# Sparse attention and a rational MLP on one core: one pool of PSUM banks, output matmuls in fours, two batches staged on 72 partitions

## The chip, the cores and the metric

The kernel runs on one core of a Trainium2 chip. The metric is the device time of one execution in microseconds. Before the change it is 473.31 us, the median of three runs (468.19 to 480.4). The core has TensorE (PE, with its weight loads as PEld), VectorE (DVE), ScalarE (ACT), GpSimd (POOL) and SyncE (SP). They run their own instruction queues in order and wait for one another on semaphores. TensorE writes to PSUM, eight banks of 512 float32 for each of 128 partitions; VectorE and ScalarE read it from there.

## The reference, cut to what matters

```python
# q, k, v: [8, 8, 576, 64]; heads 0-3 are local, heads 4-7 strided
scores = q @ k.T / sqrt(64)
mask_local   = (rel >= 0) & (rel < 32)                      # rel = query - key
mask_strided = (rel >= 0) & (query % 32 == key % 32)
attn = softmax(where(mask, scores, -1e9)) @ v               # per head
x = attn as [4608 tokens, 512]
h = x @ w_in                                                # [4608, 2048]
P = a0 + a1*h + a2*h^2 + a3*h^3
Q = 1 + |b0|*|h| + |b1|*h^2
out = (P / (Q + 1e-6)) @ w_out                              # [4608, 512], float32
```

## The kernel before

**Staging.** Each of eight batches has four local heads ("L") and four strided heads ("S"). q and k are needed with the head dimension on the partitions. For batches 2 to 7, GpSimd's queue issues DMAs that cast them into a bfloat16 copy in device memory (L391), and SyncE's queue issues transposing DMAs from there (L549). Batches 0 and 1 (`b < NPE`) take a shorter way: a casting DMA (L437) brings the raw rows into an MLP buffer h, on TP = 96 partitions of TW = 384 elements, TensorE transposes them with an identity (L489, and L520 for copies with the head halves exchanged), and ScalarE and VectorE copy the result out of PSUM (L501, L503, L532, L534). There, two neighbouring positions of the sequence share one column: 64 partitions each.

**Attention.** A batch has four units: local, strided, strided, local, two heads each. In every unit TensorE writes a mask and the scores into a pair of banks (L657 and L666 for local, L740 and L747 for strided); VectorE takes the negative maxima (L676, L754); TensorE adds them (L683, L761); ScalarE takes the exponential (L689, L767). The result P is transposed, by TensorE in batches 0 and 1 (L701, L779, copied out by L589 and L591) and by SyncE's DMA later (L707, L787). TensorE then multiplies by v into another pair of banks (L718, L804; the strided units' sums L796 go to a bank of their own), and VectorE normalises (L727, L729, L811, L815). `turn` transposes the batch's output (L615, L621), and ScalarE writes it into XT (L636), the MLP's input. In a strided unit the 36 positions of a class stand 8 columns apart in q and k, and L747 reads them with that step.

**MLP.** Tokens go in nine chunks of 512. `mlp1` makes h: 16 tiles of four matmuls (L840), each evicted by ScalarE (L846), in two groups of eight tiles. Nine VectorE instructions on 128 x 4096 elements (L858 to L880) and a logarithm and exponential on ScalarE (L863, L865) turn a group into P/Q. `mlp2` multiplies by w_out: four output tiles m, for each a step of eight matmuls per group (L903), then an eviction (L914; two of the last chunk's by L912) and a store (L921) from GpSimd's queue, in the last chunk from SyncE's.

**Order.** The code makes a list of operations with an engine, a planned duration and a key. `schedule` is a greedy planner: it gives each engine the ready operation with the lowest key. `emit` writes the order out with semaphores, so on the chip it is fixed. Attention's key is 576 b + 144 per unit, mlp1's 512 c + 1500 (1000 for c = 0) + 16 per tile, mlp2's 512 c + 2250 + 60 m.

**PSUM.** The eight banks are dealt out by purpose in rings, in program order: R_ps, two pairs, for scores and accumulators of attention and the transposes of staging (the last chunk's outputs too); R_ph, two banks, for mlp1 and the transposes of P; R_sm, one bank, for sums and `turn`; R_po, one bank, for mlp2. A ring's next tile waits until the tile of the same place is free.

Of the kernel before, what the change touches and what calls it, by code (L numbers as in the profile page):

```python
# [22 lines left out]
class Op:  # L23

    __slots__ = ("eng", "maker", "dur", "deps", "key", "dst", "dma", "gen", "ndep", "users",
                 "ready", "fin", "cnt", "idx", "know")
# [33 lines left out]

class Prog:
    ENG = ("pe", "act", "dve", "pool", "sp")
# [5 lines left out]
    def op(self, eng, maker, dur, key, r=(), w=(), m=(), dma=None, after=()):  # L68
        o = Op(eng, maker, dur, key, None, dma)
        o.idx = len(self.ops)  # L70
        for d in after:
            o.deps[d] = 1
        for t in r:
            for d in t.w:
                o.deps[d] = 1
        for t in w:
            for d in t.prev:
                o.deps[d] = 1
        for t in m:
            for d in t.w + t.r:  # L80
                o.deps[d] = 1
        for t in r:
            t.r.append(o)
        for t in w:
            t.w.append(o)
        for t in m:
            t.w = [o]
            t.r = []
        if dma is not None:
            assert len(w) == 1  # L90
            o.dst = w[0]
            o.gen = w[0].gen
            o.dst.ndma[o.gen] = o.dst.ndma.get(o.gen, 0) + 1
        o.deps.pop(o, None)
        self.ops.append(o)
        return o

    def schedule(self):
# [13 lines left out]
        left = len(self.ops)  # L112
        while left:
# [14 lines left out]
            _, _, o = heapq.heappop(avail[e])  # L128
            free[e] = t + o.dur
# [8 lines left out]
            left -= 1  # L138
            for u in o.users:
                lat = 0.07 if u.eng == o.eng else 0.15  # L140
# [101 lines left out]
def bass_strided_sparse_attn__then__act_rational_pade_kernel(nc, q, k, v, moe_w_in, moe_w_out, moe_a, moe_b, out):  # L242
# [8 lines left out]
    CH = 512  # L251
# [11 lines left out]
    TP = 96  # L263
# [56 lines left out]
    R_o = ring("os", 3, [128, Fout], f32)  # L320


    def ps(name, shape):
        return nc.alloc_psum_tensor(name, shape, f32)
    R_ps = Ring([Tile(f"ps{i}", ps(f"ps_s{i}", [128, 2, 512])) for i in range(2)])
    R_ph = Ring([Tile(f"ph{i}", ps(f"ps_h{i}", [128, 512])) for i in range(2)])
    R_sm = Ring([Tile("sm0", ps("ps_sm", [128, 512]))])
    R_po = Ring([Tile("po0", ps("ps_out", [128, 512]))])

# [142 lines left out]
    def loads_pe(b, key, tq, tk, after):  # L472
        for n in range(2):
            h = stage[b, n]
            hv = h.t[:, :, :].rearrange("p g c -> p (g c)")
            for i, (t, st_) in enumerate(((tq, T_q[b][n]), (tk, T_k[b][n]))):
                eng = ("act", "dve")[i]
                sl = R_ps.next()
                pv = sl.t.bitcast(bf)
# [3 lines left out]
                def tr(e, pv=pv, hv=hv, i=i):  # L483
                    r = None
                    for hh in range(HL):
# [5 lines left out]
                P.op("pe", tr, 1.2, key + 2 * n, r=[st_, h, T_c], w=[sl], after=after)  # L491

                def ev(e, pv=pv, t=t, n=n, eng=eng):
                    o = t.t[:, PRE + n * SW:PRE + n * SW + SW].rearrange(
                        "p (a h q j) -> p a h q j", a=2, h=2, j=NB)
                    r = None
                    for a in range(2):
                        oo = o[:, a]
                        ii = pv[:, a, 0:2 * SC].rearrange("p (h j q) -> p h q j", h=2, j=NB)
                        if eng == "act":  # L500
                            r = e.activation(oo, ii, AF.Copy)  # L501
                        else:
                            r = e.tensor_copy(oo, ii)  # L503
# [6 lines left out]
                sw = (R_po, R_sm)[i].next()  # L510
                sv = sw.t.bitcast(bf)

                def tr2(e, sv=sv, hv=hv, i=i):
                    r = None
                    for x in range(2):
                        for hh in range(2):
                            for j in range(NB):
                                c0 = (i * HL + 2 * x + hh) * TW + 128 * j + 64 * (1 - x)
                                o0 = hh * SC + TP * j
                                r = e.transpose(sv[64 * x:64 * x + 64, o0:o0 + TP], hv[0:TP, c0:c0 + 64],  # L520
                                                IDN[0:TP, 0:TP])
                    return r
                P.op("pe", tr2, 0.8, key + 1, r=[st_, h, T_c], w=[sw], after=after)

                def ev2(e, sv=sv, t=t, eng=eng):
                    r = None
                    for x in range(2):
                        d0 = 0 if x else PRE + 2 * SW
                        oo = t.t[64 * x:64 * x + 64, d0:d0 + PRE].rearrange("p (h q j) -> p h q j", h=2, j=NB)
                        ii = sv[64 * x:64 * x + 64, 0:PRE].rearrange("p (h j q) -> p h q j", h=2, j=NB)  # L530
# [56 lines left out]
    def evict(eng, o, i, dur, key, src, dst):  # L587
        if eng == "act":
            P.op("act", lambda e: e.activation(o, i, AF.Copy), dur, key, r=[src], w=[dst])  # L589
        else:  # L590
            P.op("dve", lambda e: e.tensor_copy(o, i), dur, key, r=[src], w=[dst])  # L591
# [15 lines left out]
    def turn(b, kind, src, key):  # L607
        for kk in range(2):
            sm = R_sm.next()
            sv = sm.t.bitcast(bf)  # L610
            if kind == "L":
                def tr(e, sv=sv, kk=kk):
                    r = None
                    for i in range(NR2):
                        r = e.transpose(sv[:, 128 * i:128 * i + 128], src.t[:, i, 128 * kk:128 * kk + 128], IDN[:, :])  # L615
                    return r
            else:
                def tr(e, sv=sv, kk=kk):
                    r = None
                    for i in range(NBK):  # L620
# [4 lines left out]
            for t0, t1 in cuts(b):  # L625
# [3 lines left out]
                if kind == "L":  # L629
                    i_ = sv[:, s0:s1].rearrange("p (j q c) -> p j c q", q=2, c=32)  # L630
                    o_ = XT[:, kk, c0:c0 + t1 - t0].rearrange("p (j c q) -> p j c q", q=2, c=32)
                else:
                    i_ = bass.AP(tensor=sv, offset=s0 // 16,
                                 ap=[[1024, 128], [1, (s1 - s0) // 16], [NR, NBK], [64, 2]])
                    o_ = XT[:, 2 + kk, c0:c0 + t1 - t0].rearrange("p (i k q) -> p i k q", k=NBK, q=2)
                P.op("act", lambda e, i_=i_, o_=o_: e.activation(o_, i_, AF.Copy), 0.25 + (t1 - t0) / 1000, key,  # L636
                     r=[sm], w=tiles)

    def attention(b, st):
# [5 lines left out]
        for kind, idx in (("L", 0), ("S", 0), ("S", 2), ("L", 1)):  # L645
            key = base + 144 * u
            u += 1
            sc = R_ps.next()
            pst = sc.t
            ng = R_ng.next()  # L650
            if kind == "L":
# [3 lines left out]
                def score(e, tq=tq, tk=tk, pst=pst, idx=idx):  # L655
# [19 lines left out]
                flat = pst[:, :, 0:W].rearrange("p a (r c) -> p a r c", c=KW)  # L675
                P.op("dve", lambda e, flat=flat, ng=ng: e.tensor_reduce(  # L676
                    ng.t[:, 0:2 * NR2].rearrange("p (a r) -> p a r", a=2), flat, axis=AX.X, op=Alu.max, negate=True),
                    1.2, key, r=[sc], w=[ng])

                def negm(e, ng=ng, pst=pst):  # L680
                    r = None
                    for j in range(2):
                        r = e.matmul(pst[:, j, 0:W], IDN[:, :],  # L683
# [6 lines left out]
                    pp.t[:, :, 0:KW].rearrange("p (a r) c -> p a r c", a=2), flat, AF.Exp, scale=0.125),  # L690
                    1.0, key, r=[sc], w=[pp])
                pt = R_ptL.next()
                if b < NPE:
                    for j in range(2):
                        ph = R_ph.next()
                        pv = ph.t.bitcast(bf)

                        def trp(e, pv=pv, pp=pp, j=j):
                            r = None
                            for i in range(NR2):  # L700
# [4 lines left out]
                              pv[0:KW, 0:128 * NR2], 0.7, key, ph, pt)  # L705
# [5 lines left out]
                acc = R_ps.next()  # L711

                def av(e, pt=pt, acc=acc, idx=idx):
                    r = None
                    for jj in range(2 * NR2):
                        par, r2 = jj % 2, jj // 2
                        for j in range(2):
                            r = e.matmul(acc.t[64 * par:64 * par + 64, j, 65 * r2:65 * r2 + 65],  # L718
# [6 lines left out]
                a4 = acc.t[:, :, 0:65 * NR2].rearrange("p a (r c) -> p a r c", c=65)  # L725
                r4 = rc.t[:, 0:2 * NR2].rearrange("p (a r) -> p a r", a=2).unsqueeze(3)
                P.op("dve", lambda e, r4=r4, a4=a4: e.reciprocal(r4, a4[:, :, :, 64:65]),  # L727
                     0.25, key, r=[acc], w=[rc])
                P.op("dve", lambda e, r4=r4, a4=a4, idx=idx: e.tensor_tensor(  # L729
                    xl.t[:, :, :].rearrange("p r (a x d) -> p x a r d", a=2, d=64)[:, idx], a4[:, :, :, 0:64],  # L730
# [6 lines left out]
            def score(e, tq=tq, tk=tk, idx=idx, pst=pst):  # L737
                r = None
                for j in range(2):
                    e.matmul(pst[:, j, 0:WS], IDN[:, :], MS[:, :], start=True, stop=False,  # L740
                             skip_group_check=True)
                for sl in range(NBK):
                    for j in range(2):
                        for par in range(2):
                            ap = [[QW, 64], [NBK, SB]]
                            off = 64 * par * QW + PRE + SW + (idx + j) * SC + 4 * (sl % 2) + sl // 2
# [6 lines left out]
            s4 = pst[0:NR, :, 0:WS].rearrange("p j (b c) -> p j b c", c=SB)  # L753
            P.op("dve", lambda e, s4=s4, ng=ng: e.tensor_reduce(  # L754
                ng.t[0:NR, :].rearrange("p (j b) -> p j b", j=2), s4, axis=AX.X, op=Alu.max, negate=True),
                0.85, key, r=[sc], w=[ng])

            def negm(e, ng=ng, pst=pst):
                r = None
                for j in range(2):  # L760
                    r = e.matmul(pst[0:NR, j, 0:WS], IDN[0:NR, 0:NR],  # L761
# [6 lines left out]
                pp.t[0:NR, :, 0:SB].rearrange("p (j b) c -> p j b c", j=2), s4, AF.Exp, scale=0.125),  # L768
                0.75, key, r=[sc], w=[pp])
            pt = R_ptS.next()  # L770
            if b < NPE:
                for j in range(2):
                    ph = R_ph.next()
                    pv = ph.t.bitcast(bf)

                    def trp(e, pv=pv, pp=pp, j=j):
                        r = None
                        for i in range(4):
# [6 lines left out]
                          pv[:, 0:512], 0.6, key, ph, pt)  # L785
# [5 lines left out]
            acc = R_ps.next()  # L791
            sm = R_sm.next()

            def av(e, pt=pt, acc=acc, sm=sm, idx=idx):
                for s8 in range(NBK):
                    e.matmul(sm.t[:, 2 * s8:2 * s8 + 2], pt.t[:, s8, :], ONE[:, :], start=True, stop=True,  # L796
                             skip_group_check=True)
                r = None
                for j in range(2):
                    for g in range(4):  # L800
                        for par, mm in ((0, 64), (1, SB)):
                            for x in range(2):
                                c0 = 64 * (4 * j + g)
                                r = e.matmul(acc.t[64 * par:64 * par + mm, x, c0:c0 + 64],  # L804
# [4 lines left out]
            P.op("pe", av, 0.75, key, r=[pt, vS, T_one], w=[acc, sm])  # L809
            rc = R_rc.next()  # L810
            P.op("dve", lambda e, rc=rc, sm=sm: e.reciprocal(rc.t[0:NR, 0:16], sm.t[0:NR, 0:16]),  # L811
                 0.25, key, r=[sm], w=[rc])
            for j in range(2):
                h = idx + j
                P.op("dve", lambda e, rc=rc, acc=acc, h=h, j=j: e.tensor_tensor(  # L815
                    xsb.t[0:NR, :, 64 * h:64 * h + 64].rearrange("p (x g) d -> p x g d", x=2),
                    acc.t[0:NR, :, 256 * j:256 * j + 256].rearrange("p x (g d) -> p x g d", g=4),
                    rc.t[0:NR, 8 * j:8 * j + 8].rearrange("p (g x) -> p x g", x=2).unsqueeze(3).broadcast_to(
# [7 lines left out]
    def mlp1(c):  # L826
# [4 lines left out]
        for g in range(NG):  # L831
            h = R_h.next()
            for f in range(g * G, g * G + G):
                ph = R_ph.next()
# [156 lines left out]
```

## Time and profile before

The profiled execution took 466.26 us, of which the span, from its first to its last instruction, is 464.5 us.

| stretch, us | PE busy | DVE busy | ACT busy | DMA engines' busy share |
|---|---|---|---|---|
| 0 to 15 | 4.82 | 6.47 | 3.84 | 1.19 |
| 15 to 30 | 11.30 | 5.43 | 4.11 | 1.27 |
| 30 to 45 | 10.68 | 6.67 | 5.41 | 1.38 |
| 45 to 60 | 13.65 | 4.87 | 8.84 | 1.12 |
| 75 to 90 | 10.91 | 12.91 | 8.97 | 0.01 |
| 90 to 105 | 11.93 | 13.21 | 7.36 | 0.10 |
| 105 to 120 | 15.00 | 6.07 | 7.93 | 0.97 |
| 165 to 180 | 12.79 | 7.58 | 6.60 | 0.94 |
| 210 to 225 | 12.80 | 10.64 | 10.11 | 1.16 |
| 285 to 300 | 14.48 | 14.93 | 8.97 | 0.24 |
| 390 to 405 | 13.68 | 14.89 | 11.61 | 0.13 |

Each row is a window of 15 us with the busy time of the engines inside it. A DMA share over 1 comes from packets that overlap on an engine. In the page, a line such as "ng L754 <- PE ps_s L747: 8.6, 5, 3.3" means that an engine stood idle before line 754 until line 747 of TensorE had ended: 8.6 us in all, 5 times, 3.3 at the longest.

### The profile page before, as it was taken

The numbers are of one execution on the slowest core, as the hardware profiler recorded it, in microseconds if no ns is written. First come the engines' busy times: TensorE is split into PE (matmuls) and PEld (weight loads), VectorE is DVE, ScalarE is ACT, GpSimd is POOL, SyncE is SP. The second block draws the span as 40 slices with busy tenths as digits, with TensorE's granted clock in tenths as the row PEclk, the third lists the DMA queues.
The fourth block names the chain that finished last, engine by engine and source line by source line (L and its number), as shares of the span: only waits on it lengthen the run. The fifth ranks groups of instructions, "written<-read, shape, count | busy, mean of one in ns | idle before, by whom it ended". The sixth has DMA issues, their size and how long they took to land.

```text
span 464.5 us, 8489 instructions
## 1 busy us (share of the span) xinstructions
PE 382.7 (82%) x3752; PEld 193.5 (42%) x3752; DVE 358.6 (77%) x311; ACT 283.8 (61%) x308; POOL 71.8 (15%) x112
## 2 busy tenths in 40 slices
PE   3586959589967979979699899899979788987970
PEld 2354424355425535535354444444434333433430
DVE  3443298982977939996879689979988989999940
ACT  3223684745655828567386677769578588788520
POOL 9921010001311111211022003101000000100100
PEclk9999997669978979999899799989989899999996
DMA  9999982019998997899997546210400010100101
GB/s 115 207 191 216 187 146 53 1 24 165 155 147 170 182 168 147 167 173 122 109 164 152 103 88 126 75 24 24 97 23 24 23 45 7 63 23 24 65 22 73
DMA packets 101829, 47.46 MB, mean 102 GB/s; under 512 B 88512, under 2 KB 97728, under 8 KB 101312
## 3 DMA queue, kind: packets, MB, share of 16 engines
q0 software_dynamic: 20384, 27.04, 31.3%
q1 hardware_dynamic: 81408, 19.87, 26.4%
q8 instruction: 29, 0.48, 0.4%
q14 instruction: 8, 0.07, 0.1%
HBM read 40.18 MB, written 18.28 MB: 126 GB/s over the span
## 4 chain that ended last, share of the span: by engine, by line
DVE 37%; PE 33%; ACT 14%; DMA 7%; SPq 3%; issue 3%; POOL 1%; DVEq 0%; POOLq 0%
PE ps_h L840 14%; DVE u L862 6%; PE ps_out L903 5%; DVE z L870 4%; DVE z L868 4%; ACT u L865 4%; ACT u L863 4%; DVE u L860 3%; DVE z L858 3%; DVE h L880 3%; DVE z L866 3%; DMA tk<-tk 3%; DVE z L869 2%; PE ps_s L747 2%; ACT h L846 2%
## 5 line engine op out<-in xcount | busy, mean ns | idle before, releaser
L840 PE MATMUL ps_h<-XT,Win 128*128 128x512 bf16 x576 | 149.6, 409 | 12.5 <-ACT h L846 11.8
L846 ACT ACTIVATE h<-ps_h 128x512 bf16<-128x512 f32 x144 | 84.3, 600 | 63.5 <-PE ps_h L840 63.3
L903 PE MATMUL ps_out<-Wout,h 128*128 128x512 bf16 x512 | 119.4, 382 | 3.6 <-ACT os L914 3.6
L840 PEld LDWEIGHTS ps_h<-XT,Win 128*128 128x128 bf16 x576 | 53.7, 103 | 86.7 <-ACT h L846 26.5
L903 PEld LDWEIGHTS ps_out<-Wout,h 128*128 128x128 bf16 x512 | 49.3, 99 | 63.0 <-ACT os L914 6.1
L863 ACT ACTIVATE u<-u,consts 128x4096 bf16<-128x4096 bf16 x18 | 66.7, 3703 | 8.0 <-DVE u L862 8.0
L921 POOL DMA_DIRECT2D out_dram<-os x32 | 24.7, 771 | 265.9 <-ACT os L914 262.0
L865 ACT ACTIVATE u<-u 128x4096 bf16<-128x4096 bf16 x18 | 65.3, 3625 | 0.0
L858 DVE TENSOR_SCALAR z<-h 128x4096 uint16<-128x4096 uint16 x18 | 22.0, 1223 | 27.1 <-ACT h L846 27.1
L870 DVE TENSOR_TENSOR z<-z,h 128x4096 bf16<-128x4096 bf16 x18 | 41.1, 2282 | 0.5
L868 DVE TENSOR_TENSOR z<-z,h 128x4096 bf16<-128x4096 bf16 x18 | 41.1, 2283 | 0.4
L862 DVE TENSOR_TENSOR u<-u,z 128x4096 bf16<-128x4096 bf16 x18 | 41.0, 2277 | 0.3
L880 DVE TENSOR_TENSOR h<-z,u 128x4096 bf16<-128x4096 bf16 x17 | 38.9, 2287 | 0.8 <-ACT u L865 0.5
L914 ACT ACTIVATE os<-ps_out 128x512 f32<-128x512 f32 x32 | 19.3, 603 | 26.6 <-PE ps_out L903 26.6
L636 ACT ACTIVATE XT<-ps_sm 128x576 bf16<-128x576 bf16 (+2 forms) x40 | 21.4, 560 | 17.3 <-PE ps_sm L621 9.5
L676 DVE TENSOR_REDUCE ng<-ps_s 128x10 bf16<-128x960 f32 x16 | 18.5, 1154 | 14.9 <-PE ps_s L666 14.9
L689 ACT ACTIVATE pL<-ps_s 128x960 bf16<-128x960 f32 x16 | 15.5, 970 | 20.0 <-PE ps_s L683 20.0
L860 DVE TENSOR_SCALAR u<-z,coef 128x4096 bf16<-128x4096 bf16 x18 | 24.2, 1344 | 0.4
L866 DVE TENSOR_SCALAR z<-h,coef 128x4096 bf16<-128x4096 bf16 x18 | 24.0, 1335 | 0.3
L869 DVE TENSOR_SCALAR z<-z,coef 128x4096 bf16<-128x4096 bf16 x18 | 23.1, 1281 | 0.4
L871 DVE TENSOR_SCALAR z<-z,coef 128x4096 bf16<-128x4096 bf16 x18 | 23.0, 1278 | 0.3
L747 PE MATMUL ps_s<-tk,tq 64*36 64x36 bf16 x512 | 20.7, 245 | 0.0
(74 smaller groups left out, 365.2 us busy)
## 6 DMA issues: line engine op xcount, KB each, us to landing
out_dram<-os POOLq DMA_DIRECT2D x32, 256.0 KB, 2.5
q<-in_q_dram POOLq DMA_DIRECT2D x12, 288.0 KB, 5.1
k<-in_k_dram POOLq DMA_DIRECT2D x12, 288.0 KB, 6.5
vS<-in_v_dram POOLq DMA_DIRECT2D x16, 144.0 KB, 7.6
vL<-v SPq DMA_DIRECT2D x24, 96.0 KB, 4.3
Win<-in_moe_w_in_dram POOLq DMA_DIRECT2D x8, 256.0 KB, 11.5
Wout<-in_moe_w_out_dram POOLq DMA_DIRECT2D x4, 512.0 KB, 22.4
v<-in_v_dram POOLq DMA_DIRECT2D x6, 288.0 KB, 5.9
```

The lines of the kernel that those rows point to most:

```text
L840: r = e.matmul(ph.t[:, :], Win[:, kk, f * 128:(f + 1) * 128], XT[:, kk, xc:xc + CH], start=(kk == 0), stop=(kk == NK1 - 1))
L846: P.op("act", lambda e, f=f, ph=ph, h=h: e.activation(h.t[:, f % G, :], ph.t[:, :], AF.Copy), 0.6, key, r=[ph], w=[h])
L858: dv(lambda e, hh=h.t, zz=z.t: e.tensor_scalar(zz.bitcast(u16)[:, :, :], hh.bitcast(u16)[:, :, :], 0x7FFF, None, op0=Alu.bitwise_and), ts ...
L860: dv(lambda e, zz=zz, uu=uu: e.tensor_scalar(uu, zz, b1_ap, b0_ap, op0=Alu.mult, op1=Alu.add), ts + 0.28, r=[z, T_b], w=[u])
L862: dv(lambda e, zz=zz, uu=uu: e.tensor_tensor(uu, uu, zz, op=Alu.mult), tt, r=[z], m=[u])
L863: P.op("act", lambda e, uu=uu: e.activation(uu, uu, AF.Ln, bias=eps1, scale=1.0), 0.833 * W / 1000 + 0.28, key, r=[T_co], m=[u])
L865: P.op("act", lambda e, uu=uu: e.activation(uu, uu, AF.Exp, scale=-1.0), 0.833 * W / 1000 + 0.19, key, m=[u])
L866: dv(lambda e, zz=zz, hh=hh: e.tensor_scalar(zz, hh, a_ap[3], a_ap[2], op0=Alu.mult, op1=Alu.add), ts + 0.28, r=[h, T_co], m=[z])
L868: dv(lambda e, zz=zz, hh=hh: e.tensor_tensor(zz, zz, hh, op=Alu.mult), tt, r=[h], m=[z])
L870: dv(lambda e, zz=zz, hh=hh: e.tensor_tensor(zz, zz, hh, op=Alu.mult), tt, r=[h], m=[z])
L880: dv(lambda e, zz=zz, hh=hh, uu=uu: e.tensor_tensor(hh, zz, uu, op=Alu.mult), tt, r=[z, u], m=[h])
L903: r = e.matmul(pot, h.t[:, j, m * 128:(m + 1) * 128], Wout[:, kk, :], start=(kk == 0), stop=(kk == NF - 1))
```

## The change

- **One pool.** PSUM is one tensor. A tile of the new class `PTile` says only its kind and how many banks it needs: "at" (attention and staging, two neighbouring banks), "ph", "sm", "po" (one each). It has no bank until the planner orders its first operation. Quotas limit the open tiles: three at, three ph, two sm, four po. If there is no room, the operation is set aside until a tile closes, and another is ordered. The new holder's first operation waits for all operations of the bank's last holder.
- **Outputs in fours.** `mlp2` cuts each group of eight into two steps of four matmuls, and its four output tiles are separate tiles from the start. The steps of one tile keep their order.
- **72 partitions.** Staging of batches 0 and 1 uses TP = 72, so TW = 512 and a row of a transpose covers four columns (NB = 4 instead of 3). For the strided half the copy out of PSUM sorts columns by class, so that L747 reads 36 neighbouring columns in these two batches.
- **Smaller edits.** The strided sums are a step of their own. L815 is cut by bank (x) and not by head (j). The ring of output buffers os has four instead of three. L840 waits for the former users of h itself. Some planned durations are changed, and the planned latency between operations of one engine is 0 instead of 0.07.

The diff, cut:

```diff
+class PTile(Tile):
+    def __init__(self, kind, need):
+        Tile.__init__(self, kind)
+        self.need = need
+        self.banks = None
+        self.ops = []
+        self.left = 0
...
+    QUOTA = {"at": 3, "ph": 3, "sm": 2, "po": 4}
...
+        def room(o, t):
+            want = [p for p in o.pts if p.banks is None]
+            if not want:
+                return t
+            if any(nopen[p.name] + 1 > self.QUOTA[p.name] for p in want):
+                return None
+            n = want[0].need
+            assert len(want) == 1
+            spots = [list(range(i, i + n)) for i in range(9 - n) if not any(held[i:i + n])]
+            if not spots:
+                return None
+            if want[0].name in ("at", "ph") and 8 - sum(held) - n < 1 and nopen["po"] + nopen["sm"] < 1:
+                return None
+            when = [max(bank_free[i] for i in b) for b in spots]
+            at = min(when)
+            if at > t + 1e-9:
+                return at
...
+            for p in want:
+                p.banks = late
+                nopen[p.name] += 1
+                for i in p.banks:
+                    held[i] = True
+                    if bank_tile[i] is not None:
+                        for d in bank_tile[i].ops:
+                            o.deps[d] = 1
+                    bank_tile[i] = p
+            return t
...
             _, _, o = heapq.heappop(avail[e])
+            at = room(o, t)
+            if at is None:
+                o.ready = max(o.ready, t)
+                blocked.append(o)
+                continue
+            if at > t:
+                heapq.heappush(pend[e], (at, o.key, o.idx, o))
+                continue
...
-                lat = 0.07 if u.eng == o.eng else 0.15
+                lat = 0.0 if u.eng == o.eng else 0.15
...
-    TP = 96
+    TP = 72
...
-    R_o = ring("os", 3, [128, Fout], f32)
-    R_ps = Ring([Tile(f"ps{i}", ps(f"ps_s{i}", [128, 2, 512])) for i in range(2)])
-    R_ph = Ring([Tile(f"ph{i}", ps(f"ps_h{i}", [128, 512])) for i in range(2)])
-    R_sm = Ring([Tile("sm0", ps("ps_sm", [128, 512]))])
-    R_po = Ring([Tile("po0", ps("ps_out", [128, 512]))])
+    R_o = ring("os", 4, [128, Fout], f32)
+    PTile.PS = nc.alloc_psum_tensor("PSUM", [128, 8 * 512], f32)
+    PTile.PSB = PTile.PS.bitcast(bf)
...
+                            if n:
+                                o2 = oo[:, hh * SC:hh * SC + SC].rearrange("p (z j i) -> p z j i", z=2, j=NB)
+                                i2 = ii[:, hh * SC:hh * SC + SC].rearrange("p (j i z) -> p z j i", z=2, j=NB)
...
-                            ap = [[QW, 64], [NBK, SB]]
-                            off = 64 * par * QW + PRE + SW + (idx + j) * SC + 4 * (sl % 2) + sl // 2
+                            n = 4 * (sl % 2) + sl // 2
+                            ap = [[QW, 64], [1 if b < NPE else NBK, SB]]
+                            off = 64 * par * QW + PRE + SW + (idx + j) * SC + n * (SB if b < NPE else 1)
...
-                o = P.op("pe", mm, 0.9, key, r=[xt, T_win[f // G]], w=[ph])
+                o = P.op("pe", mm, 0.9, key, r=[xt, T_win[f // G]], w=[ph], after=h.prev)
...
+        for h, p0, p1, tp in groups:
+            for p in range(p0, p1, 4):
+                parts.append((h, p, min(p + 4, p1), tp))
+        groups = parts
+        pos = [PTile("po", 1) for m in range(CH // 128)]
```

## The prediction, as it was put on record

> **What bounds the kernel now.** I read the page's totals first (VectorE's row is its busy tenths in 40 slices), then the busy time by stretch.
>
> ```profile
> span 464.5 us, 8489 instructions
> ...
> PE 382.7 (82%) x3752; PEld 193.5 (42%) x3752; DVE 358.6 (77%) x311; ACT 283.8 (61%) x308; POOL 71.8 (15%) x112
> ...
> DVE  3443298982977939996879689979988989999940
> ```
>
> ```profile
> 0.00:55.10 55.10, 36.91 (x442) 22.63 (x443) 18.58 (x38) 18.13 (x28) 26.80 (x45) 1.00 1.25 183
> 55.10:445.00 389.90, 338.74 (x3279) 167.78 (x3278) 337.51 (x271) 264.49 (x278) 44.95 (x67) 0.92 0.51 93
> 445.00:464.50 19.50, 7.08 (x32) 3.05 (x32) 2.53 (x4) 1.19 (x2) 0.00 (x0) 0.78 0.14 54
> ```
>
> In the stretch rows the fourth and fifth figures are TensorE's and VectorE's load and busy time as PEld and DVE: VectorE works 18.6, 337.5 and 2.5 us. Its polynomial rows cannot shrink here, so I do the bookkeeping on VectorE: span = 358.6 busy + 105.9 idle, and the idle splits into 36.5 (start, 55.1 - 18.6), 52.4 (middle, 389.9 - 337.5) and 17.0 (end). The change touches no polynomial instruction; its worth is the idle that it removes.
>
> Next the waits, asked for VectorE from 105 to 270 us, and the rows of VectorE's timeline with long gaps (bracket: idle before, and who ended it).
>
> ```profile
> DVE ng L676 <- PE ps_s L666: 12.0, 6, 4.4
> DVE ng L754 <- PE ps_s L747: 8.6, 5, 3.3
> DVE z L858 <- ACT h L846: 6.1, 5, 1.8
> DVE rc L811 <- PE ps_s L804: 5.5, 3, 2.6
> DVE rc L727 <- PE ps_s L718: 4.9, 4, 2.9
> ```
>
> ```profile
> 55.10 1.23 DVE L858 TENSOR_SCALAR z<-h 128x4096 uint16<-128x4096 uint16 x1 [13.11 <-ACT h L846]
> ...
> 114.03 1.16 DVE L676 TENSOR_REDUCE ng<-ps_s 128x10 bf16<-128x960 f32 x1 [3.99 <-PE ps_s L666]
> ```
>
> These five add to 37.1 us: VectorE starves on attention results between 105 and 270. The same question for 270 to 445 gives 9.6 us at L858 and 0.5 at L880; the remaining 5.2 of the 52.4 are small gaps and the stretch 55 to 105. Ending the start is the first L858, at 55.10. So three places: the start, 105 to 270, and a little later on.
>
> **The start.** Timeline, attention of batch 0:
>
> ```profile
> 17.41 0.99 PE L666 MATMUL ps_s<-tk,tq 64*32 64x96 bf16 x36
> ...
> 18.45 1.16 DVE L676 TENSOR_REDUCE ng<-ps_s 128x10 bf16<-128x960 f32 x1 [0.31 <-PE ps_s L666]
> ...
> 20.68 0.97 ACT L689 ACTIVATE pL<-ps_s 128x960 bf16<-128x960 f32 x1 [4.36 <-PE ps_s L683]
> ...
> 22.80 0.68 PE L740 MATMUL ps_s<-MS,IDN 128*128 128x288 bf16 x2
> ...
> 23.42 1.29 PE L747 MATMUL ps_s<-tk,tq 64*36 64x36 bf16 x32
> ```
>
> R_ps has two pairs, handed out in program order score, accumulator, score, accumulator. So the next unit's score (L740, 22.80) needs the pair that the exponential L689 leaves at 21.65, though TensorE had ended its score at 18.40. With up to three pairs given out by need, that score can start some 4.4 us earlier. From 16.48 to the first L840 at 44.96 are 28.5 us; TensorE's groups in it add to 22.7 (two local units of 5.0, two strided of 4.75, four turns of 3.15 in all). So 5.8 us is all that overlap can take at this matmul pace. The class-ordered half adds to that: L747 takes 1.29 per 32 matmuls here and also at 209.94, whatever the pace; L804, with unit step and the same 32 matmuls, takes 0.64 at the slow pace and 0.44 at the fast one. Two scores lie in the start: 2 x 0.65 = 1.3. Upper end: if TensorE stays busy, its pace doubles (a group of four 128x512 needs 0.43 us per matmul at 45 us and 0.216 at 51), which adds perhaps 2. I take -5, ends +1 and -9.
>
> **Staging on 72 partitions.** The columns streamed stay (16 x 72 = 12 x 96); the transposes go from 144 to 192. A group of 12 takes 1.14 slow or 0.68 fast, so each costs 0.057 to 0.095: the 48 new ones cost between 0 (column-bound) and 4.6 us in all, half of it in the start, where TensorE waits 2.13 us for h at 13.98 anyway. Evicting the strided half takes four instructions of 288 instead of two of 576, eight more in all; the fixed part is bounded by the smallest PSUM row (reciprocal, 217 ns): four on VectorE, +0.9. Four transfers of h carry the same 288 KB in 288 rows instead of 384. The first landed 6.75 us after issue (1.30 to 8.05); fewer, longer rows could save up to a quarter, fewer partitions cost up to a third of what moves: -1 to +2 on the path. I take +1 for all of this.
>
> [...]
>
> **105 to 270.** Not all of the 37.1 is open to banks. TensorE itself waits for transposing DMAs in that stretch: tk at L657 7.7, P at L796 3.5, tk at L740 2.7, about 14, and DMA is 0.84 to 1.16 busy in most of those windows. That part stays. 23 is open: between 105 and 118, VectorE idles 9 us because batch 1's attention ended late (its last turns at 104) and chunk 1's mlp1 only then could start. Its units queue on two pairs as batch 0's did, and L740 waits 2.4 us for L689 at 70.4. Earlier attention also issues the next loads earlier: POOL stands from 69 to 107 at an output store (38.06 us, ended by L914), while DMA share is 0.01 to 0.10 from 75 to 105; splitting mlp2 in fours and giving it more banks releases that store and what is queued behind it. Batch 1's two contiguous scores save 1.3 more. I take two thirds, -15; ends +5 and -23.
>
> **270 to 445.** TensorE waits 29.7 us for mlp1's banks (20.0 load + 9.7 matmul, L840 behind L846) and 9.4 for the only output bank (L903 behind L914). Three ph banks and up to four output banks cover most of it, but VectorE is 94% busy, so only its 10.1 us of waits can go. I take -4, ends 0 and -10.
>
> **End and rest.** The last L912 waits 1.63 us for an os buffer; a fourth removes it, and next the last of four store issues (3.19 us together from 451.45) is late: -1, ends 0 and -1.6. L815 regrouped keeps 32 instructions of 512 elements (682 ns), the sums as their own step keep their matmuls: 0. L840 now waits for the old users of h on TensorE; the eviction L846 waited for them already, and the last of them are TensorE's own L903: 0, cover lost only if an h buffer is short, in which case attention queued behind L840 waits too, with VectorE after it. Fours add boundaries, not steps. [...]
>
> Sum: -5 + 1 - 15 - 4 - 1 = -24. Span 440.5, with the 1.76 outside it (466.26 - 464.5) 442.3. The profiled run lies 1.5% under the median of 473.31; scaled the sum would be 449. I predict 446. Own range: all lower ends (-9 -1 -23 -10 -1.6) give an own time of 421.7, all upper ends (start +1, staging +2 DMA +2.3 transposes +0.9 evictions, middle +5) 477.5; I take 424 to 464 of it.
>
> **Rivals.**
> - *Output banks starve attention (slower).*
>
> ```profile
> 78.39 1.89 PE L903 MATMUL ps_out<-Wout,h 128*128 128x512 bf16 x8
> ...
> 104.65 1.46 PE L903 MATMUL ps_out<-Wout,h 128*128 128x512 bf16 x6
> ```
>
> Today the single output bank sits half summed for 26 us, until the second group's h is there. The planner fills any idle TensorE time with what is ready, so all four output tiles can be opened with the first group, and four banks stay held. Four remain: one pair for attention if mlp1 takes two. Then units run one after the other: the first local unit takes 16.48 to 26.53, the first strided 22.80 to 32.27, so four take 39 us against 28.5, +10.5 a batch. For it: the hold and the greedy plan. Against: attention ranks ahead of the same period's output steps, and from batch 2 on P's transposes need no banks. Two batches cancel the gain of 24; from three on it is slower: four give 464.5 + 42 - 24 = 482.5, scaled about 491. Chance 0.18.
> - *DMA and VectorE hold the middle (no change).* If 105 to 270 is set by loads, -15 becomes 0 to -5 and the sum is -9 to -14: 452 to 457, scaled 459 to 464; with the start not gained either, 470. For it: the DMA windows. Against: the DMA hole at 75 to 105. Chance 0.22, of which 0.04 still counts as over 2%.
> - *The plan is not what the chip does.* Banks change hands by planned durations; where an eviction is late, TensorE stands with all queued behind it, giving back what the third pair gives. This lies inside +5 at the middle term: about 465 to 475, within 2%. Chance 0.02.
>
> **How the numbers follow.** Forecast 0.58. A difference under 2% cannot be told from none. Faster 0.58 + 0.04 = 0.62, within 2% 0.20, slower 0.18. Range 424 to 480: it leaves out most of the slower rival and the case of every gain at its end.
>
> **What would show it.** First L858 near 50 instead of 55; L740 of the second unit before L689 of the first; L747 of batches 0 and 1 at 0.5 to 0.7 us per 32; VectorE's waits from 100 to 270 near 20 us; the last L912 without a DMA wait. It is wrong if the output bank's first and second four are 15 us apart on four tiles at once while L676 waits for L666, or if h lands later than 8 us.

## The result and the profile after

The changed kernel takes 440.14 us (median of four runs, 435.48 to 441.54), where the kernel before takes 472.0 (four runs, 468.19 to 480.4). The ratio is 0.9333, 95% interval 0.9227 to 0.9439. The forecast was 446, a ratio of 0.942 to the first median of 473.31. The two profiled runs took 466.26 and 441.54. Single runs of one program lie up to 15 us apart in this study, so whole times are compared by ratios of the means of the fast runs with their intervals, and traces by places that repeat.

The page's totals of the changed kernel, in the columns of before:

```profile
span 439.8 us, 8607 instructions
...
PE 368.9 (84%) x3800; PEld 186.4 (42%) x3800; DVE 361.0 (82%) x315; ACT 284.7 (65%) x312; POOL 69.9 (16%) x112
...
DVE  3471799999983257899999999999999999999930
```

VectorE works 2.4 us more than before, so its idle time fell by 27.1 us for a span that is 24.7 shorter. The row of tenths shows where it stands idle now: at the start, once around the 13th to 15th slice (132 to 165 us), and at the end. Three stretches follow: up to the first L965, the first VectorE instruction on a group (L858 before), called the first product below; from there to the start of the last 32 output matmuls; and the rest. In each row the third pair of figures after the length is VectorE's busy time:

```profile
0.00:46.62 46.62, 30.69 (x488) 18.41 (x489) 18.38 (x40) 17.86 (x31) 27.22 (x45) 0.93 1.40 170
46.62:418.83 372.21, 328.97 (x3287) 164.40 (x3283) 340.08 (x273) 265.68 (x280) 42.66 (x67) 0.94 0.57 103
418.83:439.80 20.97, 9.27 (x32) 3.59 (x32) 2.53 (x4) 1.19 (x2) 0.00 (x0) 0.66 0.14 51
```

VectorE's idle time is the length less the busy time. The end begins with the last 32 output matmuls, at 445.0 before and 418.83 after:

| VectorE, us | before | after | difference |
|---|---|---|---|
| busy | 358.6 | 361.0 | +2.4 |
| idle in the start | 36.5 | 28.2 | -8.3 |
| idle in the middle | 52.4 | 32.1 | -20.3 |
| idle at the end | 17.0 | 18.4 | +1.5 |

**The start.** Rows of batch 0 on TensorE (PE) and ScalarE (ACT):

```profile
15.31 0.99 PE L765 MATMUL PSUM<-tk,tq 64*32 64x96 bf16 x36
...
17.14 0.99 PE L765 MATMUL PSUM<-tk,tq 64*32 64x96 bf16 x36
...
19.08 0.97 ACT L788 ACTIVATE pL<-PSUM 128x960 bf16<-128x960 f32 x1 [7.17 <-PE PSUM L782]
...
24.67 0.42 PE L841 MATMUL PSUM<-MS,IDN 128*128 128x288 bf16 x2 [0.37 <-DVE tk L601]
...
25.02 0.57 PE L849 MATMUL PSUM<-tk,tq 64*36 64x36 bf16 x32
...
26.01 0.57 PE L849 MATMUL PSUM<-tk,tq 64*36 64x36 bf16 x32
```

The second unit's score (17.14) no longer waits for the first one's exponential (19.08). The planner chose the other local unit, whose operands need only the first half of q and k. The strided scores read neighbouring columns and take 0.57 us where they took 1.29. TensorE is also at its faster pace by then: the mask matmuls L841 take 0.42 us where L740 took 0.68. And attention begins 2.1 us earlier, at 14.40 (L756) instead of 16.48 (L657), because the transposes of the strided half, at 13.98 and 15.56 before, now come behind it, at 20.62 and 22.34.

**The middle.** VectorE's waits from 100 to 270 us, and its busy time in five stretches:

```profile
DVE ng L856 <- PE PSUM L849: 14.4, 2, 10.3
DVE rc L919 <- PE PSUM L899: 6.4, 2, 4.5
DVE rc L827 <- PE PSUM L818: 3.4, 3, 2.0
DVE ng L775 <- PE PSUM L765: 2.4, 2, 1.9
DVE xS L922 <- PE PSUM L912: 0.2, 1, 0.2
```

```profile
46.62:96.50 49.88, 42.51 (x561) 23.53 (x558) 48.67 (x48) 36.15 (x44) 1.54 (x3) 0.93 0.60 102
96.50:120.00 23.50, 23.50 (x254) 12.44 (x253) 23.22 (x19) 15.64 (x16) 5.68 (x9) 1.00 0.88 166
120.00:161.50 41.50, 29.61 (x403) 16.29 (x405) 19.66 (x24) 19.02 (x26) 7.01 (x12) 0.75 1.04 152
161.50:261.50 100.00, 94.58 (x1102) 48.56 (x1103) 93.57 (x78) 74.59 (x81) 15.51 (x24) 0.97 0.88 150
261.50:420.00 158.50, 139.95 (x987) 64.01 (x986) 156.10 (x109) 120.27 (x116) 12.92 (x19) 0.96 0.20 52
```

The waits add to 26.8 us where they were 37.1. Of the third stretch's 41.5 us VectorE works 19.7: 21.8 of the 32.1 idle us lie there. The five idle times are 1.2, 0.3, 21.8, 6.4 and 2.4 us. Stretches of the same lengths before, from 55.1 on, had 4.0, 9.0, 10.5, 18.6 and (270 to 445) 10.3. So the 9 us at 105 to 118 are gone, the last two fell from 28.9 to 8.8, and one new hole of 11 us more has opened. What made it:

```profile
137.56 0.60 ACT L953 ACTIVATE h<-PSUM 128x512 bf16<-128x512 f32 x1 [0.19 <-PE PSUM L947]
144.37 0.64 PE L841 MATMUL PSUM<-MS,IDN 128*128 128x288 bf16 x2 [6.84 <-DMA tk<-k]
...
146.27 0.76 DVE L856 TENSOR_REDUCE ng<-PSUM 100x16 bf16<-100x576 f32 x1 [10.26 <-PE PSUM L849]
```

TensorE reaches L841 in its fixed order and waits 6.84 us there for a transposing DMA of k, issued at 126.20. mlp1's next tiles are queued behind it, so ScalarE and VectorE stand too. On GpSimd's queue the next loads no longer follow an output store, but they wait too:

```profile
100.57 0.49 POOL L482 DMA_DIRECT2D q<-in_q_dram  x1 [29.47 <-DMA ptL<-pL]
```

**The end.**

```profile
404.04 9.83 PE L1013 MATMUL PSUM<-Wout,h 128*128 128x512 bf16 x32 [8.77 <-DVE h L987]
...
418.83 9.27 PE L1013 MATMUL PSUM<-Wout,h 128*128 128x512 bf16 x32 [4.96 <-DVE h L982]
426.84 0.60 ACT L1025 ACTIVATE os<-PSUM 128x512 f32<-128x512 f32 x1 [10.61 <-PE PSUM L1013]
427.27 0.69 DVE L1023 COPY os<-PSUM 128x512 f32<-128x512 f32 x1 [7.30 <-PE PSUM L1013]
...
428.13 0.69 DVE L1023 COPY os<-PSUM 128x512 f32<-128x512 f32 x1 [0.17 <-PE PSUM L1013]
```

The last copy (428.13) waits for no store any more. But TensorE, which had finished the output matmuls that were ready, stands idle 8.8 and 5.0 us, and its last 32 matmuls take 9.27 us instead of 7.08.

### The profile page after: what moved, and what is told of

It reads as the page before. It is cut to its first block, busy times and chain, and to the rows that moved or that the text cites. A ratio compares the mean times of both kernels' runs of the same rounds, so it can differ in the third digit from the quotient of the medians.

```text
span 439.8 us, 8607 instructions
## 1 busy us (share of the span) xinstructions
PE 368.9 (84%) x3800; PEld 186.4 (42%) x3800; DVE 361.0 (82%) x315; ACT 284.7 (65%) x312; POOL 69.9 (16%) x112
## 4 chain that ended last, share of the span: by engine, by line
DVE 49%; PE 17%; DMA 13%; SPq 9%; ACT 6%; issue 3%; DVEq 0%; POOLq 0%
DVE u L969 7%; DVE z L977 6%; PE PSUM L947 5%; DVE h L987 5%; DMA tk<-k 5%; PE PSUM L1013 4%; DMA ptS<-pS 4%; DVE z L975 4%; DVE u L967 4%; DVE z L965 4%; SPq L674 3%; DVE z L978 3%; DVE z L976 3%; DVE z L973 3%; DVE xS L922 3%
## 5 line engine op out<-in xcount | busy, mean ns | idle before, releaser
L1013 PE MATMUL PSUM<-Wout,h 128*128 128x512 bf16 x576 | 139.3, 394 | 16.9 <-DVE h L987 9.8
L947 PE MATMUL PSUM<-XT,Win 128*128 128x512 bf16 x576 | 139.3, 388 | 4.2 <-ACT h L953 2.6
L953 ACT ACTIVATE h<-PSUM 128x512 bf16<-128x512 f32 x144 | 83.0, 603 | 39.3 <-PE PSUM L947 39.0
L1013 PEld LDWEIGHTS PSUM<-Wout,h 128*128 128x128 bf16 x576 | 56.2, 101 | 86.4 <-DVE h L987 9.6
L947 PEld LDWEIGHTS PSUM<-XT,Win 128*128 128x128 bf16 x576 | 53.3, 100 | 72.3 <-ACT h L953 11.5
L972 ACT ACTIVATE u<-u 128x4096 bf16<-128x4096 bf16 x18 | 65.1, 3619 | 0.4
L969 DVE TENSOR_TENSOR u<-u,z 128x4096 bf16<-128x4096 bf16 x18 | 41.2, 2291 | 0.5
L1025 ACT ACTIVATE os<-PSUM 128x512 f32<-128x512 f32 x34 | 19.3, 599 | 25.6 <-PE PSUM L1013 25.6
L965 DVE TENSOR_SCALAR z<-h 128x4096 uint16<-128x4096 uint16 x18 | 21.8, 1212 | 12.5 <-ACT h L953 12.5
L735 ACT ACTIVATE XT<-PSUM 128x576 bf16<-128x576 bf16 (+2 forms) x40 | 19.8, 556 | 11.1 <-PE PSUM L719 8.1
L788 ACT ACTIVATE pL<-PSUM 128x960 bf16<-128x960 f32 x16 | 15.5, 967 | 14.8 <-PE PSUM L782 14.8
L482 POOL DMA_DIRECT2D q<-in_q_dram x12 | 6.6, 548 | 110.5 <-DMA ptL<-pL 73.5
L856 DVE TENSOR_REDUCE ng<-PSUM 100x16 bf16<-100x576 f32 x16 | 11.9, 750 | 14.4 <-PE PSUM L849 14.4
```

Of the source, the lines that this page charges most:

```text
L947: r = e.matmul(ph.f, Win[:, kk, f * 128:(f + 1) * 128], XT[:, kk, xc:xc + CH], start=(kk == 0), stop=(kk == NK1 - 1))
L953: P.op("act", lambda e, f=f, ph=ph, h=h: e.activation(h.t[:, f % G, :], ph.f, AF.Copy), 0.6, key, r=[ph], w=[h])
L965: dv(lambda e, hh=h.t, zz=z.t: e.tensor_scalar(zz.bitcast(u16)[:, :, :], hh.bitcast(u16)[:, :, :], 0x7FFF, None, op0=Alu.bitwise_and), ts ...
L969: dv(lambda e, zz=zz, uu=uu: e.tensor_tensor(uu, uu, zz, op=Alu.mult), tt, r=[z], m=[u])
L972: P.op("act", lambda e, uu=uu: e.activation(uu, uu, AF.Exp, scale=-1.0), 0.833 * W / 1000 + 0.19, key, m=[u])
L1013: r = e.matmul(po.f, h.t[:, j, m * 128:(m + 1) * 128], Wout[:, kk, :], start=(kk == 0), stop=(kk == NF - 1))
```

## The experiments

The first idea, called A, was that the gain comes from handing banks out as matmuls are ordered; the rival, B, that it comes from the number of tiles that may be open. "Middle" below is VectorE's idle time from the first product (its first L965) to the start of the last output matmuls, and "end" is its idle time after that, in the profiled run of each. Ratios are to the kernel before, with a 95% interval in brackets. No run undoes the changed planned durations and latency by themselves.

**Old counts, given out as ordered.**

```diff
-    QUOTA = {"at": 3, "ph": 3, "sm": 2, "po": 4}
+    QUOTA = {"at": 2, "ph": 2, "sm": 1, "po": 1}
```

> The changed kernel with the quotas cut to the counts of the old rings (two at pairs, two ph, one sm, one po); banks are still given out as matmuls are ordered, and all other edits stay. Theory A (it is the order of handing out, not the number: a score no longer stands behind its predecessor's accumulator): most of the gain stays, ratio to before 0.94 to 0.96, first L965 at 47 to 50 us. Rival B (it is the number of open tiles, above all the third pair): the gain goes, ratio 0.98 to 1.01, first L965 at 53 us or later.

Ratio 0.986 (0.967 to 1.004), unclear. First L965 at 45.93, middle 53.0, end 22.0. Its profiled run took 467.22, 9 us above its fastest, so the middle is a high reading. The two ideas split the kernel between them: the start is A's, in full and with two pairs; the whole time is nearer B's, though the interval is wide.

**Two pairs only.** Quota of at 2, the others as changed.

> Only the quota of at tiles is cut, from three to two pairs; ph, sm and po keep three, two and four. Theory A: ratio 0.935 to 0.95. Rival B: 0.965 or more, with VectorE's idle time before L775 and L856 back above 20 us.

Ratio 0.963 (0.949 to 0.977). First L965 at 46.02, middle 42.1. Just under B's bound; L775 and L856 had 30.2 us of waits, as B said, 16 of them in one hole. In that hole TensorE stood 10.5 us at L841 for a transposing DMA of k, as in the changed kernel's hole, so this run by itself does not show that the third pair is what was missing.

**One output bank.** Quota of po 1, the others as changed.

> Only the quota of output tiles is cut, from four to one. If the output banks' early opening is worth something in the middle (it empties h and lets output stores go early): ratio 0.945 to 0.96. If it is worth nothing, or takes banks from attention as the slower rival of the prediction had it: 0.92 to 0.935. The cold end of the changed kernel (32 matmuls in 9.27 us after 418.8) should go back to about 7.1 us if the early output matmuls are its cause.

Ratio 0.981 (0.971 to 0.992). First L965 at 46.02, middle 43.0, end 23.7. The output banks are worth something, more than was expected. In the changed kernel all four output tiles are indeed opened with the first group, as the prediction's slower rival had it:

```profile
74.54 1.90 PE L1013 MATMUL PSUM<-Wout,h 128*128 128x512 bf16 x8
77.83 1.89 PE L1013 MATMUL PSUM<-Wout,h 128*128 128x512 bf16 x8
83.01 3.62 PE L1013 MATMUL PSUM<-Wout,h 128*128 128x512 bf16 x16
101.27 1.89 PE L1013 MATMUL PSUM<-Wout,h 128*128 128x512 bf16 x8
```

The first 32 output matmuls are done by 86.7 us; the kernel before had done eight of its first 32 at 78 and the last at 127. The half-summed tiles hold their banks for some 20 us, and VectorE idles only 1.2 us until 96.5. The expectation on the end was wrong: with one bank the last four tiles follow one another, and it is 5 us longer, not shorter.

**Staging on 96 partitions, columns in sequence order.**

```diff
-    TP = 72
+    TP = 96
...
-                            ap = [[QW, 64], [1 if b < NPE else NBK, SB]]
+                            ap = [[QW, 64], [NBK, SB]]
```

and the copies of n = 1 arranged as those of n = 0.

> Staging of batches 0 and 1 on 96 partitions and columns in sequence order again, L849 reads with a step of eight in all batches; the pool stays. Theory: four scores of 32 matmuls cost 0.7 us more each, half of them in the start; the four extra copies per engine go; net +1 to +3 us, ratio 0.935 to 0.942, first L965 1 to 2 us later. Rival (72 partitions cost in the transfers what the step saves): no difference or up to 2 us faster, ratio 0.928 to 0.934.

Ratio 0.947 (0.936 to 0.958): more than expected as a median, but the interval overlaps the changed kernel's (0.923 to 0.944), and its profiled span was even shorter (438.0). The place itself is clear: first product at 48.15, 1.5 us later, with these two scores in the start:

```profile
24.32 1.29 PE L845 MATMUL PSUM<-tk,tq 64*36 64x36 bf16 x32
...
26.14 1.29 PE L845 MATMUL PSUM<-tk,tq 64*36 64x36 bf16 x32
```

The price of 72 is clear too. Smallest, median and largest time from issue to landing of the eight staging loads, 96 partitions here and 72 in the changed kernel, both from the answer on their line:

```profile
DMA to landing us min/median/max: 6.9/11.8/17.1
```

```profile
DMA to landing us min/median/max: 7.0/14.2/20.2
```

The median is a fifth longer, but the first transfer, on which the start hangs, hardly (6.9 and 7.0). The kernel before, also on 96, had 6.7, 11.7 and 16.7.

**Output matmuls in eights.** `range(p0, p1, 8)` in place of 4.

> The changed kernel with output matmuls in steps of eight again; four output banks and all else stay. If the finer steps are worth something of their own: ratio 0.945 to 0.96. If the gain of the output side is the banks alone: 0.93 to 0.94, no more than 3 us from the changed kernel.

Ratio 0.962 (0.955 to 0.970), first L965 at 45.16, middle 43.2. By itself this says that the fours matter. But its longest wait, 13.7 us, is again a transfer's (TensorE stood 9.8 of them at L818 for a transposed P), and the controls below take most of it back.

**Last chunk's first output matmuls held back.**

```diff
+                            after=prev[m] + ([gate[2]] if last and i == 0 else []))]
```

where `gate[2]` is L969 of the last group (in the profile L972, as lines move).

> The changed kernel with one more wait: the last chunk's first 32 output matmuls wait for the last group's L969 (which ended at 408.9), so that TensorE runs without a gap into the final 32. The order of all instructions stays. Theory (the end is 1.4 us worse than before because TensorE idles 8.8 and 5.0 us and runs the last matmuls at a slow clock): the final 32 matmuls take 7.0 to 7.6 us instead of 9.27, the end from the last polynomial instruction 2 us less, ratio 0.927 to 0.931. Rival (the clock is not set by the gap): the end stays at 18.4 us of VectorE idle or grows.

```profile
418.36 9.38 PE L1016 MATMUL PSUM<-Wout,h 128*128 128x512 bf16 x32 [13.61 <-DVE u L972]
...
428.30 7.08 PE L1016 MATMUL PSUM<-Wout,h 128*128 128x512 bf16 x32 [0.56 <-DVE h L985]
```

The final 32 take 7.08 us and the end has 16.2 us of idle instead of 18.4, as was expected. Whole times of this program went from 433.84 to 448.82 (median 446.35), with the order of instructions of the changed kernel; no ratio is drawn from them. The profiled run's middle was 41.5, against 32.1, with VectorE's and ScalarE's instructions in the same order. TensorE's waits for transfers in that stretch are 23.8 us against 14.7, most of the difference at the transposed P of strided units (13.5 against 3.6): 9 of the 9.4 us between the two middles go with when transfers land.

**A nudge of the planner, upward.** The planned duration of an mlp1 tile 0.91 instead of 0.90.

> A control for how far the time moves when only the plan is another: one planned duration, that of an mlp1 tile, is 0.91 instead of 0.90; what is computed and on which banks kinds stays. If differences of the earlier runs are chance of the plan: the ratio lies 0.02 or more from 0.933. If they are due to the quotas: within 0.01 of it, 0.925 to 0.943.

Ratio 0.950 (0.939 to 0.961), first L965 at 45.31, middle 40.4: between the two expectations (0.953 or more, 0.943 or less). Another plan of the same kernel came out 1.7% off, though the two intervals just overlap; by the two traces nearly all of it is in the middle, and TensorE's waits for transfers there are 21.5 us against 14.7.

**Loads planned to land later.**

```diff
-                o.fin = dmafree[e] + 2.2
+                o.fin = dmafree[e] + (6.0 if busy else 2.2)
```

> The planner counts on 6.0 instead of 2.2 us until a DMA has landed while another queue is busy, so that what needs it is ordered later on TensorE. Theory (the largest hole left, VectorE's 10.3 us before L856 at 146, is TensorE standing in order at L841 for a load that came 18 us after its issue): the hole shrinks below 4 us and the ratio is 0.91 to 0.925. Rival (the load itself sets the pace, or the new plan opens other holes): 0.93 to 0.95.

```profile
137.42 0.76 DVE L856 TENSOR_REDUCE ng<-PSUM 100x16 bf16<-100x576 f32 x1 [4.22 <-PE PSUM L849]
```

The hole shrank from 10.3 to 4.2 us and the middle to 27.3, but the ratio is 0.936 (0.927 to 0.946): other waits of 3 to 4 us appeared (at 143.1, 147.2 and 200.9). The rival stands.

**A nudge downward.** 0.89 instead of 0.90.

> A second control of the changed kernel: the planned duration of an mlp1 tile is 0.89 instead of 0.90. The first control, 0.91, gave 0.950 where the changed kernel had 0.933. If the gain belongs to the pool and its size to the luck of the plan: 0.925 to 0.955. If the changed kernel was one lucky plan: 0.96 or more.

Ratio 0.936 (0.925 to 0.948), first L965 at 46.38, middle 34.5. The changed kernel's time does not belong to one lucky plan.

**Old counts with the upward nudge.**

> The kernel with the old counts of banks (two pairs, two ph, one sm, one po), given out as matmuls are ordered, with the planned duration of an mlp1 tile 0.91 instead of 0.90. The first plan with these counts gave 0.986. If the counts are the cause: 0.97 to 1.0, above all three plans of the changed kernel, with VectorE's first L965 at 45 to 47 and its idle time after that above 45 us. If that run was an unlucky plan: 0.96 or less.

Ratio 0.969 (0.960 to 0.977), first L965 at 45.93, middle 43.4, end 22.1. Above all three plans of the pool by ratio, though its interval touches that of the upward nudge; the ratio lies just under the expected 0.97, and the middle misses the expected 45.

**The kernel before with the upward nudge.**

> The kernel before with the same nudge of its planner, 0.91 instead of 0.90; no other edit. If the kernel before was an unlucky plan: 0.97 or less. If its place is due to the rings: 0.98 to 1.02, first L858 at 54 to 56.

Ratio 0.987 (0.975 to 0.999), first L858 at 54.53, middle 51.1, end 16.9.

**Later landings and the held output matmuls together.**

> The two edits e8 and e6 together on the changed kernel: loads planned to land later while another queue is busy, and the last chunk's first output matmuls held for L969. Theory: e8's middle (VectorE idle 27 us) with e6's end (16.2 us), ratio 0.925 to 0.935. Rival (the middle differs from execution to execution as much as these edits bring): no different from 0.936.

Ratio 0.924 (0.914 to 0.935), median 436.76 (433.26 to 440.57): the fastest kernel measured, though its interval overlaps the changed kernel's. Its end is the one expected, 16.2 us with

```profile
418.14 7.08 PE L1016 MATMUL PSUM<-Wout,h 128*128 128x512 bf16 x32 [0.44 <-DVE h L985]
```

and its middle is 31.6, not 27: only the end came out as planned.

**Taken together.** All plans of three kinds of kernel:

| kernel | ratios | first product, us | middle, us | TensorE's waits for transfers in the middle, us |
|---|---|---|---|---|
| rings | 1, 0.987 | 55.1, 54.5 | 52.4, 51.1 | 15.0, 16.0 |
| old counts, given out as ordered | 0.986, 0.969 | 45.9, 45.9 | 53.0, 43.4 | 27.7, 29.9 |
| the pool | 0.933, 0.950, 0.936 | 46.6, 45.3, 46.4 | 32.1, 40.4, 34.5 | 14.7, 21.5, 17.3 |

The means of the ratios are 0.994, 0.977 and 0.940. By them the larger counts are worth 0.037, some 18 us of 472. Giving out as ordered, together with the staging and the small edits, is worth 0.016, some 8 us, which is no more than two plans of one kind differ by; its place is clear all the same, the start. Cutting one count alone (e2, e3) or the fours (e5) gives middles of 42 to 43. By ratio only the single output bank lies clear of the pool's three plans; for the third pair and the fours the runs do not settle it.

The end is the part of the counts that repeats: 22.0, 23.7 and 22.1 us with one output bank, 18.4 to 19.1 in the pool's three plans. The middle is less sure. The last column adds up where TensorE stood until a DMA had landed, and without it 37.4 and 35.1 us are left for the rings, 25.3 and 13.5 for the old counts, 17.4, 18.9 and 17.2 for the pool. Such a difference is rough, since a wait of TensorE need not reach VectorE. Read so, giving out as ordered also shortens the middle, and what the old counts lose there is lost at transfers, above all at the transposed P of local units: 11.8 and 15.0 us, and 20.5 with one output bank, against 2.2 to 4.1 in the pool's plans. That fewer open tiles leave TensorE less to do before such a wait would explain it, but it is not shown: e6, with the pool's counts, has 23.8 us of such waits.

## Why the prediction held

**Size and sign.** The forecast sum was -24 against the profiled run's own time; the profiled span fell by 24.7. The median moved by 31.9, more than the 27 from 473.31 to the forecast of 446, with the second profile taken on the longest run of its kernel. That the sum is met within a microsecond is partly luck: the start and the time after 270 gave more than their terms, 105 to 270 gave less. Of the signs, the first product came at 46.6 instead of near 50, and VectorE's waits from 100 to 270 were 26.8 us instead of near 20. The first h was there at 8.36, later than the 8 us that were to show the forecast wrong, but it was at 8.05 before; that sign could not tell the two kernels apart.

**The start, -5.** It was -8.3, inside the ends and near the lower one. The step is right: the second score starts at 17.14, before the first exponential. Four things were mis-sized or misread. I put a third pair to it; e1 and e2 reach the first product as early with two (45.93 and 46.02), so it is the order of handing out, with the staging and the small edits, that no run takes apart further. The 22.7 us of TensorE's groups overlap one another: the profile has it busy for 20.93 of the 28.5 us, so 7.6 and not 5.8 was open. That stretch, from the first score's mask to the first mlp1, shrank by 6.0 us, the faster pace included, which the forecast had only in the -9 end of its range; attention's earlier beginning added 2.1, and stood in no term. And the contiguous scores gained 0.72 each, 1.29 to 0.57; undoing them with the rest of the staging (e4) costs 1.5 us at this place, where the sum had 1.3.

**Staging, +1.** The transposes cost next to nothing: before the first score 16 of 72 columns take 1.14 us (L580), as 12 of 96 did (L489), and for the exchanged head halves it is 0.95 (L617) against 0.86 (L520). VectorE's busy time rose by 2.4 us where 0.9 was reckoned for the extra copies. These took 0.6, as four of 751 ns became eight of 449; normalising takes what it took (683 ns against 682), and the rest is not explained. For the loads I had put -1 to +2 us on the path, shares of the first landing's 6.75 us: up to a quarter saved by fewer rows (288 for 384), up to a third lost by fewer partitions (72 for 96). Both were estimates from these ratios, and no run shows either by itself. What the runs show is the loads' median, 14.2 us against 11.8 in e4, a factor of 1.20; the path of the start does not show it, as the first landing is the same (7.0 us after issue, 6.9 in e4), and where the kernel before waits 2.13 and 0.46 us for later ones, at 13.98 and 15.56, the transposes at 20.62 and 22.34 wait for none.

**105 to 270, -15, and after, -4.** Together with what stood for small gaps it was -20.3 in the middle. By the stretches of equal length the first was only -9.5 and the second -7.9, and 55 to 105, which had no term, gave -2.8. Batch 1's attention did end earlier, its last turns at 77 instead of 104, and the 9 us at 105 to 118 are gone. What stands against them is the new hole at the load of k. One reason I gave did not work: the DMA share stays at 0.01 from 75 to 97 us. The next loads did stand behind an output store before, and go 7 us earlier now (100.57 instead of 107.60), but without the store GpSimd's queue stands 29.47 us for the first transposed P of batch 2 (L806). And what stayed is not spread thin as I had it: a third of it, 10.3 us, is one hole at a load. The waits for banks after 270 were misread as well. Their 29.7 and 9.4 us count a weight load's wait and its matmul's as two, where TensorE is idle for 18.0 us in all; the term did not rest on them, since it was bounded by VectorE's 10.1.

**The end, -1.** It was +1.5, the one term with the wrong sign. A missing os buffer was priced, and it did go; that TensorE would finish its output work early, stand idle and run its last matmuls slowly was not seen. e6 shows it: the same 32 matmuls take 7.08 us after a gap of 0.56 us, not 9.27 after 4.96. The prediction had the row for it (0.43 and 0.216 per matmul), and used it for the start alone.

**Rivals.** The slower one came true in its mechanism and not in its price: four output tiles are held half-summed for some 20 us, and VectorE idles only 1.2 us in that time, so attention does not starve. Reducing them to one bank made the kernel 3 to 5% slower than the pool's plans, not faster. The no-change rival was wrong on the middle as a whole, but transfers do own the largest hole that is left, and in e6 and e7 most of what the middle has more than the changed kernel's. That the plan is not what the chip does was given 0.02 as a rival; nudging the plan moved the time by 1.7% at most, about as much as the staging's 1.4 (e4), and neither is clear of the intervals.

## What to carry to other kernels

Look first at who waits for a buffer that the program order, not the data, gives away: a ring dealt to two uses in turn chains them, and no extra buffer was needed to undo it in the start (e1). Give the work that nobody waits for (here output matmuls) enough accumulators that it can fill gaps early, but keep some of it for the end, so that the matrix engine does not arrive idle at the last step (here its last 32 matmuls took 9.27 us after 4.96 us of idling, and 7.08 after 0.56 in e6). Where a planner fixes the order, nudge one of its numbers and measure again before believing a difference of one or two per cent, and compare how long the engines stood at transfers: that alone differed by 9 us between two runs of one order.

## What the hardware showed unexpectedly

TensorE's last 32 matmuls of 128x512 were slower after a long gap than after a short one. They took 9.27 us after a gap of 4.96 us, and 9.65 and 10.00 in e9 and e7, where its weight loads stood idle for 6.7 and 6.4 us before them (5.4 in the changed kernel); in e5 and e8 they took 9.79 and 9.92. They took 7.08 after gaps of 1.61, 0.56 and 0.44 (the kernel before, e6 and e12), and 7.08 in e11. The granted clock shows it there, 0.76 over the 9.27 us and 1.00 over the 7.08 of the kernel before and of e6, but not everywhere. In the kernel before, it reads 1.00 from 45 to 49 us, where a matmul takes 0.43:

```profile
45.00:49.00 4.00, 4.00 (x10) 1.00 1.24 245
49.00:55.00 6.00, 6.00 (x27) 1.00 1.01 177
```

Ten matmuls in 4 us against 27 in 6 us at the same figure: here the matmuls' own spacing is the better witness. In the kernel before, the strided scores do not follow that pace at all: with a step of eight elements 32 of them take 1.29 us at 23 us, where the mask before them takes 0.68, and at 210 us, where it takes 0.41. Neighbouring columns bring that to 0.57 (mask 0.42). Last, a transposing DMA issued at 126.20 landed 18 us later, where the median of its kind in that kernel is 5.5.
